# Routed attention with an FFN behind it, one core: a shorter centroid chain, the first one-hot DMAs issued earlier, and three transposes of the fourth pair moved beneath the scores

## The chip, the cores and the metric

One Trainium2 chip, one core. The metric is device time in microseconds (us), the median of several executions. The times of a trace are counted from the start of the span, which is shorter than the time (the profiled execution of the kernel before: span 344.3, time 346.12).

Engines: PE = TensorE, PEld = its weight loads, DVE = VectorE, ACT = ScalarE, POOL = GpSimd, SP = SyncE. "ACTq" and "SPq" in a profile line are issues of DMAs.

## The reference, cut to what matters

```python
batch, n_heads, seq, head_dim, n_clusters = 4, 8, 768, 64, 16
q_assign = argmax(einsum(q_n, c_n)); k_assign = argmax(einsum(k_n, c_n))   # nearest centroid
mask = q_assign[:, :, :, None] == k_assign[:, :, None, :]
attn = softmax(where(mask, scale * q @ k.T, -1e9)); x = attn @ v           # 32 heads
# then, on the 3072 x 512 rows: RMS norm, silu(x @ w_gate) * (x @ w_val) @ w_out
```

The kernel takes two heads at a time ("pairs", 16 in all). The mask is made by 16 extra rows on the contraction: a one-hot of each token's cluster is put below the 64 rows of q and k (tile `aug`, 80 partitions), so a pair's scores can't start before its one-hots are there.

## The kernel before: the parts concerned

Each pair is prepared in thirteen parts: T0 to T3 (three PE transposes each and a copy from PSUM), CAST (bf16 rows of `aug`), SP (assignment matmuls), TR, MX, CMP, SCL, BACK (the one-hot chain, all on DVE), PLACE (DMAs of the one-hots into `aug`), CASTV.

```python
    c_in = const.tile([P, D], F32, name="c_in")
    nc.scalar.dma_start(out=c_in, in_=centroids.rearrange("h c d -> (h c) d"))
    for pi in range(3):
        load_pair(pi, (0, 1))        # q and k, 384 KB each, issued by SP
    load_part(0, 2)                  # v of the first pair
    load_pair(3, (0, 1))
    # ... cut ...
        def place():                 # PLACE: 24 KB each
            ohT = state["ohT"]
            for a in range(2):
                for side in range(2):
                    # ... cut: first pair: ACT issues q's, POOL issues k's ...
                    eng.dma_start(out=aug[st][a][D:KA, side, :].rearrange("c (r n) -> c r n", r=2),
                                  in_=ohT[r:r + 2 * NC, :])
    # ... cut ...
    for i in (TR, MX, CMP, SCL, BACK):
        p0[i]()
    p1[T2](); p1[T3]()
    w_ps = keep_warm(3)              # matmuls of zeros into a scratch bank
    for i in (T0, T2):
        p2[i]()
    p0[PLACE]()
    # ... cut ...
    p3[T0]()
    p3[T1]()                         # needs the fourth pair's k
    keep_warm(2, w_ps)
    load_part(1, 2, nc.scalar)
    p1[SP](); p1[TR](); p1[CAST]()
    keep_warm(3, w_ps)
    # from here on: steps; one step = a score chunk of a head, and what at(step, ...) hangs on it
    for step in range(NT):
        score_chunk(slot, j)         # 3 banks of scores per exp at first
        # ... cut: FFN piece, attention x v, division ...
        extras(step)
```

The softmax here doesn't subtract the row's maximum and nothing guards it: scores larger than these inputs give would overflow.

## Time and profile before

| | kernel before |
|---|---|
| time | 346.56 us, median of 3 (345.97 to 346.69) |
| span of the trace | 344.3 |
| first score matmul, first exp | 16.65, 17.50 |
| first FFN matmul (`gp`) | 64.92 |
| start of the last block of output matmuls (`dp`) | 332.22 |

These four marks cut the span into three stretches. Up to the first exp, loads and preparation decide; from there to the first `gp`, ACT's exps; behind it, PE. Of the third, two waits, in the timeline of PE of the kernel before (start, length, engine, line, operation, operands, count, and in brackets the idle time ahead with its releaser):

```profile
279.50 0.81 PE L402 MATMUL gp<-xnT,wg 128*128 128x384 bf16 x4 [0.44 <-DVE uu L411]
280.62 0.81 PE L402 MATMUL vp<-xnT,wv 128*128 128x384 bf16 x4 [0.32 <-DVE gvT L417]
```

### The profile page before, as it was taken

Reading aid. Unit: us, or ns where it says so; the run is one execution under the profiler, and the core shown is the slowest. Engines: PE = TensorE matmul, PEld = TensorE weight load, DVE = VectorE, ACT = ScalarE, POOL = GpSimd, SP = SyncE. Lnnn points to the kernel's source line nnn. Section 1 sums busy time; section 2 is a strip of 40 time slices with the busy share of each in tenths; the row PEclk is TensorE's granted clock in tenths of the full one; section 3 lists DMA queues with packets and bytes.
Section 4 is the critical chain, followed back from the end, with each engine's and each line's share of the span. In section 5 each row is a group of like instructions: output and inputs, shape, how many; then the busy total and the mean of one; then the engine's idle time right before and its main releaser. Section 6 shows DMA issues by size and latency. Waiting matters only on the chain.

```text
span 344.3 us, 7504 instructions
## 1 busy us (share of the span) xinstructions
PE 332.0 (96%) x2925; PEld 202.9 (59%) x2958; DVE 222.2 (65%) x458; ACT 226.9 (66%) x391; POOL 88.9 (26%) x123
## 2 busy tenths in 40 slices
PE   8899999999999999999999999999999999999995
PEld 3446666667666565666656566666666645555553
DVE  5684788698764778866465567874554677655540
ACT  4489999978777686766767677777777253323322
POOL 2677786066431123230111205010000011000000
PEclk9999999999999999999999999999999999999999
DMA  7665999909943125161501003120000022300012
GB/s 258 211 202 166 260 239 249 267 14 152 228 150 112 69 64 166 42 183 41 170 5 42 32 12 78 38 51 32 32 24 9 32 31 77 78 30 30 32 61 91
DMA packets 36770, 34.98 MB, mean 102 GB/s; under 512 B 13520, under 2 KB 33664, under 8 KB 36736
## 3 DMA queue, kind: packets, MB, share of 16 engines
q1 hardware_dynamic: 30240, 29.20, 27.3%
q0 software_dynamic: 5984, 4.84, 9.3%
q10 hardware_dynamic: 512, 0.48, 0.5%
q8 instruction: 23, 0.38, 0.5%
q14 instruction: 11, 0.09, 0.1%
HBM read 28.61 MB, written 6.29 MB: 101 GB/s over the span
## 4 chain that ended last, share of the span: by engine, by line
PE 84%; DVE 7%; ACT 3%; DMA 3%; issue 2%; POOL 1%; POOLq 0%; DVEq 0%; SPq 0%; ACTq 0%
PE gp L402 17%; PE vp L402 17%; PE dp L435 16%; PE sc L300 12%; PE acc L314 9%; PE tp L196 5%; PE sp L232 3%; PE scw L300 2%; DMA k_in<-in_k_dram 2%; ACT pT L303 2%; PE w_ps L129 1%; DVE qk L200 1%; DVE oh L249 1%; DVE x L324 1%; DVE xn L368 1%
## 5 line engine op out<-in xcount | busy, mean ns | idle before, releaser
L303 ACT ACTIVATE pT<-sc 128x512 bf16<-128x512 f32 x192 | 113.8, 598 | 45.5 <-PE sc L300 44.9
L411 DVE SCALAR_TENSOR_TENSOR uu<-th,gp 128x384 f32<-128x384 f32 x96 | 53.0, 552 | 66.5 <-ACT th L407 66.3
L402 PE MATMUL gp<-xnT,wg 128*128 128x384 bf16 x384 | 78.1, 325 | 0.6 <-DVE uu L411 0.4
L402 PE MATMUL vp<-xnT,wv 128*128 128x384 bf16 x384 | 78.2, 326 | 0.5 <-DVE gvT L417 0.5
L407 ACT ACTIVATE th<-gp 128x384 f32<-128x384 f32 x96 | 47.2, 492 | 43.6 <-PE gp L402 41.0
L314 PEld LDWEIGHTS <-pT 128*128 128x128 bf16 x1152 | 56.8, 97 | 29.4 <-DVE x L324 2.4
L300 PE MATMUL sc<-aug 80*128 80x512 bf16 (+1 forms) x256 | 73.0, 327 | 0.0
L435 PE MATMUL dp<-wo,gvT 128*128 128x512 bf16 (+1 forms) x268 | 71.3, 369 | 1.6
L219 POOL CAST aug<-qk 64x768 bf16<-64x768 f32 x60 | 51.7, 862 | 56.3 <-DVE qk L200 38.2
L314 PE MATMUL acc<-vbf,pT 128*128 128x65 bf16 x1152 | 62.9, 194 | 1.7 <-DVE x L324 0.9
L417 DVE TENSOR_TENSOR gvT<-uu,vp 128x384 bf16<-128x384 f32 x96 | 52.6, 548 | 5.9 <-PE vp L402 0.8
L402 PEld LDWEIGHTS <-wg 128*128 128x128 bf16 x384 | 37.2, 97 | 30.7 <-issue 1.3
L402 PEld LDWEIGHTS <-wv 128*128 128x128 bf16 x384 | 37.1, 97 | 19.1 <-issue 0.9
L303 ACT ACTIVATE pT<-scw 128x1536 bf16<-128x1536 f32 x32 | 44.8, 1457 | 5.1 <-DMA v_in<-in_v_dram 2.4
L435 PEld LDWEIGHTS <-gvT 128*128 128x128 bf16 x300 | 29.1, 97 | 24.4
L300 PEld LDWEIGHTS <-aug 80*128 80x128 bf16 x384 | 33.1, 98 | 17.2 <-issue 7.1
L200 DVE COPY qk<-tp 128x384 f32<-128x384 f32 x38 | 20.7, 553 | 17.0 <-PE tp L196 16.9
L300 PE MATMUL scw<-aug 80*128 80x512 bf16 (+1 forms) x128 | 26.1, 326 | 0.4 <-issue 0.4
L359 POOL TENSOR_SCALAR ir<-ss 128x3 f32<-128x3 f32 x7 | 1.6, 235 | 95.6 <-ACT jk L345 84.0
L368 DVE SCALAR_TENSOR_TENSOR xn<-x,ir,g_b 128x512 bf16<-128x512 bf16 x24 | 20.4, 862 | 6.8 <-POOL ir L360 5.7
L224 POOL CAST vbf<-v_in 128x768 bf16<-128x768 f32 x16 | 13.6, 847 | 34.3 <-issue 33.9
L202 ACT COPY qk<-tp 128x384 f32<-128x384 f32 x26 | 12.3, 479 | 11.0 <-PE tp L196 10.8
(62 smaller groups left out, 217.2 us busy)
## 6 DMA issues: line engine op xcount, KB each, us to landing
q_in<-in_q_dram SPq DMA_DIRECT2D x16, 384.0 KB, 6.1
k_in<-in_k_dram SPq DMA_DIRECT2D x16, 384.0 KB, 6.6
out_dram<-ob SPq DMA_DIRECT2D x23, 256.0 KB, 2.0
v_in<-in_v_dram SPq DMA_DIRECT2D x15, 384.0 KB, 6.4
wg<-in_moe_w_gate_dram POOLq DMA_DIRECT2D x4, 384.0 KB, 8.7
wv<-in_moe_w_val_dram POOLq DMA_DIRECT2D x4, 384.0 KB, 11.4
wo<-in_moe_w_out_dram POOLq DMA_DIRECT2D x4, 384.0 KB, 7.6
aug<-ohT SPq DMA_DIRECT2D x57, 24.0 KB, 1.9
```

Source lines behind the costliest of these rows:

```text
L196: nc.tensor.transpose(tp[:, i * P:(i + 1) * P], src[:, a, i * P:(i + 1) * P], ident_f)
L200: nc.vector.tensor_copy(dst, tp)
L219: nc.gpsimd.tensor_copy(aug[st][a][0:D, :, par * HS:(par + 1) * HS], qk32[0][par * D:(par + 1) * D, 2 * a:2 * a + 2, :])
L300: nc.tensor.matmul(sc[:, o:o + n], lhsT=ag[:, 1, kc * P:(kc + 1) * P], rhs=ag[:, 0, qo:qo + n], start=True, stop=True)
L303: nc.scalar.activation(pts[slot][:, j * CH:(j + nch) * CH], sc[:, :nch * CH], ACT.Exp, scale=scale)
L314: nc.tensor.matmul(acc[:, TORD[g], :], lhsT=pts[slot][:, kc * S + g * P:kc * S + (g + 1) * P], rhs=vb[:, a, TORD[kc], :], start=(kc == 0), ...
L368: nc.vector.scalar_tensor_tensor(st["xn"][:, tl, :], x_t[b][:, t, :], st["ir", m][:, tl:tl + 1], g_b, op0=ALU.mult, op1=ALU.mult)
L402: nc.tensor.matmul(pt[:, :HS], lhsT=w[:, dc, fc * P:(fc + 1) * P], rhs=xnT[b, m][:, :, dc, :], start=(dc == 0), stop=(dc == DC - 1))
L407: nc.scalar.activation(th, pt[:, :HS], ACT.Tanh, scale=0.5)
L411: nc.vector.scalar_tensor_tensor(uu, th, 1.0, pt[:, :HS], op0=ALU.add, op1=ALU.mult)
L417: nc.vector.tensor_tensor(gvT[half][:, fc, :], uu, pt[:, :HS], op=ALU.mult)
L435: nc.tensor.matmul(dp, lhsT=gvT[hf][:, f, tl * P:(tl + 1) * P], rhs=wo[:, f, cols], start=(f == 0), stop=(f == FC - 1))
```

## The change

Its intent: let the first scores start earlier, and keep PE's in-order stream from standing at tiles that the scores don't need (0.51 us at the fourth pair's k tile in the trace of before). The core of the diff (cut: the dummy matmuls, who copies which tile, an extra column of 1e-15 in `c_in` for the sum of squares, the second pair's assignment and transpose, which move from ahead of the scores to step 0, and the third pair's steps, which move to 4 to 18):

```diff
-    for pi in range(3):
+    for pi in range(4):
         load_pair(pi, (0, 1))
     load_part(0, 2)
-    load_pair(3, (0, 1))
@@ centroid chain
-    nc.vector.tensor_mul(c_sq, c_in, c_in)
-    nc.vector.reduce_sum(c_ss, c_sq, axis=AX)
+    nc.vector.scalar_tensor_tensor(c_sq, c_in, 1.0, c_in, op0=ALU.mult, op1=ALU.mult, accum_out=c_ss)
     nc.vector.reciprocal(c_t, c_nm)
-    nc.vector.tensor_mul(c_t, c_t, c_ss)
-    nc.vector.tensor_add(c_nm, c_nm, c_t)
-    nc.vector.tensor_scalar(c_nm, c_nm, scalar1=0.5, scalar2=1e-6, op0=ALU.mult, op1=ALU.add)
-    nc.vector.reciprocal(c_t, c_nm)
-    for i in range(2):
-        nc.vector.tensor_scalar_mul(c2[:, i, :], c_in, c_t)
+    nc.vector.scalar_tensor_tensor(c_t, c_t, c_ss, c_nm, op0=ALU.mult, op1=ALU.add)
+    nc.vector.tensor_scalar_add(c_t, c_t, 2e-6)
+    nc.vector.reciprocal(c_t, c_t)
+    nc.vector.tensor_scalar_mul(c2, c_in[:, 0:D].unsqueeze(1).to_broadcast([P, 2, D]), c_t)
@@ ahead of the scores
-    for i in (T0, T1, T2, T3):
-        p0[i]()
-    put_centroids()
-    p0[CAST]()
+    p0[T0]()
+    p0[T2]()
+    keep_warm(2, w_ps)
+    put_centroids()
+    p0[T1]()
+    p0[T3]()
+    p0[CAST]()
+    for i in (SP, TR, MX, CMP, SCL, BACK, PLACE):
+        p0[i]()
     p3[T0]()
-    p3[T1]()
-    p1[SP]()
-    p1[TR]()
@@ steps
-    for i, step in ((T2, 4), (T3, 7), (SP, 11), (TR, 13), ...):           # p3
+    for i, step in ((T1, 10), (T2, 12), (T3, 15), (SP, 19), (TR, 20), ...):
@@ last batch's RMS norm
-            early = (8, 8, 8, 9, 9, 10, 11) if b == B - 1 else ...
+            early = (8, 8, 9, 9, 10, 11, 12) if b == B - 1 else ...
@@ weight loads
-    for i, step in enumerate((44, 49, 54, 60, 66, 71, 75, 77, 105, 111, 117, 123)):
+    for i, step in enumerate((44, 49, 54, 59, 64, 67, 70, 72, 105, 111, 117, 123)):
```

More of the change, by code (lines that the diff above doesn't have):

```diff
@@ L89, in load_pair @@
             load_part(pi, kind)
-    c_in = const.tile([P, D], F32, name="c_in")
-    nc.scalar.dma_start(out=c_in, in_=centroids.rearrange("h c d -> (h c) d"))
-    for pi in range(3):
+    c_in = const.tile([P, D + 1], F32, name="c_in")
+    nc.vector.memset(c_in[:, D:D + 1], 1e-15)
+    nc.scalar.dma_start(out=c_in[:, 0:D], in_=centroids.rearrange("h c d -> (h c) d"))
+    for pi in range(4):
         load_pair(pi, (0, 1))
     load_part(0, 2)
-    load_pair(3, (0, 1))
     g_b = const.tile([P, DM], F32, name="g_b")
@@ L130, in keep_warm @@
         return w_ps
-    c_sq = const.tile([P, D], F32, name="c_sq")
+    c_sq = const.tile([P, D + 1], F32, name="c_sq")
     c_ss = const.tile([P, 1], F32, name="c_ss")
@@ L191, in t_group @@
                 tp = ((ps_t, ps_pv)[g - 2]).tile([P, HS], F32, name="tp", tag=("t", "acc")[g - 2])
+            elif (pi, g) in late:
+                tp = late[pi, g][:, 0:HS]
             else:
@@ L197, in t_group @@
             dst = qk32[0][:, g, :]
-            on_dve = (g % 2 == 0 if pi == 0 else g > 1 if pi in (1, 3) else g % 2 if pi == 2 else pi < 7 or g % 2)
+            on_dve = (g in (0, 3) if pi == 0 else g == 3 if pi == 2 else pi < 7 or g % 2)
             if on_dve:
@@ L206, in casts @@
             if pi == 0:
-                for g in range(4):
+                for g in (0, 2, 1, 3):
                     a, side = divmod(g, 2)
@@ L471 @@
     p0, p1, p2, p3 = (prep_parts(pi) for pi in range(4))
-    keep_warm(8)
-    for i in (T0, T1, T2, T3):
-        p0[i]()
-    put_centroids()
-    p0[CAST]()
-    keep_warm(3)
-    p0[SP]()
-    p1[T0]()
-    p1[T1]()
-    for i in (TR, MX, CMP, SCL, BACK):
-        p0[i]()
-    p1[T2]()
-    p1[T3]()
-    w_ps = keep_warm(3)
-    for i in (T0, T2):
-        p2[i]()
-    p0[PLACE]()
-    p0[CASTV]()
-    for i in (T1, T3):
-        p2[i]()
-    keep_warm(2, w_ps)
+    w_ps = keep_warm(8)
+    p0[T0]()
[5 more added lines that the diff above has]
+    p0[CAST]()
+    keep_warm(1, w_ps)
+    for i in (SP, TR, MX, CMP, SCL, BACK, PLACE):
+        p0[i]()
+    for i in (T0, T1, T2, T3):
+        p1[i]()
+    late[3, 0] = keep_warm(3)
+    for i in (T0, T2, T1, T3):
+        p2[i]()
     p3[T0]()
-    p3[T1]()
-    keep_warm(2, w_ps)
     load_part(1, 2, nc.scalar)
-    p1[SP]()
-    p1[TR]()
     p1[CAST]()
-    keep_warm(3, w_ps)
+    keep_warm(4)
     first.close()
@@ L503 @@
                                                  reuse_waits="tile"))
-    for i, step in ((MX, 0), (CMP, 1), (SCL, 1), (BACK, 2), (PLACE, 2), (CASTV, 3)):
+    at(2, p0[CASTV])
+    for i, step in ((SP, 0), (TR, 0), (MX, 1), (CMP, 2), (SCL, 2), (BACK, 3), (PLACE, 3), (CASTV, 5)):
         at(step, p1[i])
-    at(3, lambda: load_part(2, 2))
-    at(5, lambda: load_part(3, 2))
+    for i, step in ((T1, 10), (T2, 12), (T3, 15), (SP, 19), (TR, 20), (MX, 21), (CMP, 22), (SCL, 23), (BACK, 24),
+                    (PLACE, 24), (CAST, 24), (CASTV, 28)):
+        at(step, p3[i])
+    for i, step in ((SP, 4), (TR, 5), (MX, 10), (CMP, 12), (SCL, 15), (BACK, 18), (PLACE, 18), (CAST, 6), (CASTV, 14)):
+        at(step, p2[i])
+    for pi in range(2, 4):
+        at(3, lambda pi=pi: load_part(pi, 2))
     at(8, lambda: load_pair(4))
-    for i, step in ((CAST, 3), (SP, 0), (TR, 3), (MX, 5), (CMP, 6), (SCL, 8), (BACK, 9), (PLACE, 9), (CASTV, 10)):
-        at(step, p2[i])
     at(22, lambda: load_pair(5))
@@ L521 @@
         else:
-            early = (8, 8, 8, 9, 9, 10, 11) if b == B - 1 else (9, 9, 10, 11, 12, 13, 15)
+            early = (8, 8, 9, 9, 10, 11, 12) if b == B - 1 else (9, 9, 10, 11, 12, 13, 15)
             plan = [(sumsq, early[:3], (0, 1, 2)), (inv, early[3:4], (0,)), (norm, early[4:], (0, 1, 2)),
@@ L527 @@
                 at(H * NCH * (b + 1) + step, lambda fn=fn, it=it, more=more: fn(it, *more))
-    for i, step in ((T2, 4), (T3, 7), (SP, 11), (TR, 13), (MX, 14), (CMP, 15), (SCL, 16), (BACK, 18), (PLACE, 18),
-                    (CAST, 18), (CASTV, 28)):
-        at(step, p3[i])
     at(30, lambda: load_pair(6))
```

## The prediction

> **What bounds the kernel now.** I read the page first, then the chain of waits that ended last, then the timeline of the first 18 us, then the ACT timeline up to 68 us, then the end (266 to 298 us). The page's part 1 gives the two busiest engines:
>
> ```profile
> PE 332.0 (96%) x2925; PEld 202.9 (59%) x2958; DVE 222.2 (65%) x458; ACT 226.9 (66%) x391; POOL 88.9 (26%) x123
> ```
>
> PE is busy for 96% of the span, but that is an average. Most of the change lies before the first scores, and there the chain in order of time shows something else:
>
> ```profile
> 6.54 7.43 DMA k_in<-in_k_dram
> ...
> 13.97 0.14 issue
> 14.11 0.52 PE tp L196 x3
> 14.63 0.43 PE w_ps L129 x2
> 15.06 0.85 PE sp L232 x8
> ```
>
> (Columns: start us, length us, what.) The end of the kernel is tied to the arrival, at 13.97 us, of the fourth pair's k tile. PE takes its instructions in order, so its transposes of that tile, some dummy matmuls [...] and the second pair's assignment all stand ahead of the first score. The timelines show the same wait from ACT's and PE's side:
>
> ```profile
> 14.11 0.52 PE L196 MATMUL tp<-ident_f,k_in 128*128 128x128 f32 x3 [0.51 <-DMA k_in<-in_k_dram]
> 15.78 0.82 PE L129 MATMUL w_ps<-zeros 128*128 128x512 bf16 x3
> 16.65 0.81 PE L300 MATMUL scw<-aug 80*128 80x512 bf16 x4
> ...
> 17.50 1.45 ACT L303 ACTIVATE pT<-scw 128x1536 bf16<-128x1536 f32 x1 [2.35 <-DMA v_in<-in_v_dram]
> ```
>
> The bracket names a v load as ACT's releaser, but that load is only issued by ACT; the exp needs the score matmuls that began at 16.65, so I read it as "waits for PE". From there to 65 us there is a second regime, bound by ACT, with 32 exps of 1.4 us almost back to back (columns: start, length, groups, idle before):
>
> ```profile
> 17.50 5.68 ACT L303 ACTIVATE pT<-scw 128x1536 bf16<-128x1536 f32 x4 [2.35 <-DMA v_in<-in_v_dram]
> 23.88 8.30 ACT L303 ACTIVATE pT<-scw 128x1536 bf16<-128x1536 f32 x6 [0.70 <-PE scw L300]
> 32.43 4.45 ACT L303 ACTIVATE pT<-scw 128x1536 bf16<-128x1536 f32 x3 [0.24 <-PE scw L300]
> ```
>
> The holes are 0.70 once and about 0.25 us per two or three heads' exps. After 65 us PE is the bound and its order is fixed, so what is won before the first exp should reach the end, if ACT stays fed and nothing waits for the weights.
>
> [...] PE stands 0.51 us for the fourth k tile although the first pair's one-hots do not need it. [...] So issuing the fourth pair's q and k ahead of v should bring them about one tile earlier. The trace has 320 to 396 GB/s from 5 to 11 us; by that, a 384 KB tile takes some 1.05 us, and the last two arrivals that PE waited for (13.05 and 13.97) are 0.92 apart, which fits. [...] The trace has 2.4 to 2.8 us from issue to landing for the first pair's 24 KB one-hots. [...] The 128x1 steps of the centroid chain take 150 to 160 ns, and start every 0.20 us, so each one removed is worth 0.20.
>
> **The change, part by part.**
>
> Centroid chain. Now: square 3.08, sum 3.34, POOL's power 3.71 to 4.27, then five steps of 0.20 us from 4.30, and two multiplications (0.42) that end at 5.70. After: square and sum in one (I estimate 0.3 from the row of 0.23 and a short accumulator read), which takes away about 0.2; one step fewer after the power, 0.20; the two multiplications as one 128x128, an estimate of 0.27 for 0.42, 0.15. Sum 0.55: the scaled centroids are ready at 5.15 instead of 5.70. PE reaches the centroid transpose at 4.69 + two groups of three transposes (0.39 and 0.33) + two dummies (0.43) = 5.84, against 6.21 now. The transpose takes 0.27, the copies to the block-diagonal tile follow at 6.19 and 6.48 and end at 6.77 (now 7.14).
>
> But this 0.37 isn't passed on. DVE must then copy T3 (k of the pair's second head), whose transposes now stand behind the centroids on PE: 6.28 to 6.77, the copy 6.81 to 7.33, then two casts of 0.56 each to 8.45. The first stream transpose of the one-hot chain starts behind these: 8.47, where it now starts at 8.32. The chain behind it lasts 8.32 to 11.03 = 2.71 us, so the one-hots are ready at 11.18 instead of 11.03. I count the shorter chain as a loss of 0.15 by itself: it pays for the rearrangement.
>
> One-hot DMAs ahead of ACT's copies. ACT now issues its two at 11.56, behind two copies that began at 11.17; after, at 11.22. POOL issues at 11.34 now (0.31 behind the one-hots), 11.49 after. With the 2.8 us to landing that the first POOL one took, the first head's rows are there at 14.0 (ACT) and 14.3 (POOL). In the kernel before they were there at about 14.4, over 2 us ahead of the scores at 16.65: this was hidden. It becomes the bound now.
>
> Three transposes of the fourth pair beneath the scores. Only T0 (q, first head) stays ahead of them. PE after: assignment to about 8.1; second pair's transposes, held by its k tile until 8.97, and three dummies to 10.65; third pair's q to 11.3; its k only once DVE has copied the second pair's first tile (DVE now copies all four, from 11.2), so 11.85 to 12.5; the fourth pair's q, which comes before v in the queue and should be there at about 12 to 12.5; then four dummies of 0.216. PE is ready at 13.7. ACT, which copies three tiles of the third pair behind its two DMA issues (1.3 us, to 12.5), needs 3 x 0.48 and is done at 13.95; the first scores' PSUM banks need one of these copies. So three arrivals: 13.7 PE, 13.95 ACT, 14.3 DMA. The latest decides; with a little for the wait itself the first score matmul begins at 14.4 and the first exp 0.85 later (16.65 to 17.50 now): 15.3. That is 17.50 - 15.3 = 2.2 us won.
>
> From 15 to 65 us. The three transposes and copies (0.33 us of PE, 0.55 of DVE each) are now done between the scores, with two 3-bank score buffers of slack. Taken off that stretch: the transposes at steps 4 and 7, behind which the second exp row stood 0.70 us idle. Put in: T1, T2 and T3 at steps 10, 12, 15, each of which needs the single transpose bank that DVE must first have emptied. I expect 0.3 of the 0.70 to remain: 0.4 won. The weight loads are issued up to five steps earlier, as they must; the eight that the first FFN pieces need landed by about 71 us, chunk by chunk ahead of their use, and no PE wait names them. I count 0.
>
> The end. The last batch's third sum of squares and the norms come one step later, so one more DVE step is done before DVE stands 1.69 us for POOL's power. PE now loses 0.44 + 0.32 us there (gp at 279.50, vp at 280.62). One wait should go, but two norms of 0.75 now follow each other directly and another should come. I count 0.
>
> Sum: 346.56 - 2.2 - 0.4 = 343.96, say 343.9 us.
>
> **The rivals.** First, that the one-hot chain is the bound and later than I think: if a 0.55 us copy more lies ahead of the stream transpose on DVE, or POOL's DMA takes 3.3 us (the longest of those seen in the first 20 us), either makes the first exp about 0.5 later, both together 16.3 and the result 344.9. For it: DVE is 93% busy or more from 5 to 12 us. Against: its order is known and I counted it.
>
> Second, that ACT's regime absorbs it. The second pair's one-hots must land before the seventh exp; I put their transpose at 18.5 and their landing at 21 to 22.6, while the scores want them at about 22.3. POOL now has the second pair's casts and a v cast (four of 0.86 and 0.84) ahead of those DMAs. If they are late, ACT stands. This would cost up to 1 us: 345.
>
> Third, that more is won: PE's in-order blocking is also what makes the 0.70 and some of the 0.25 holes, and the end may lose its 0.76. All of it would make 342.8.
>
> Fourth, that the loads are what ends last anyway: if the fourth q tile still lands at 13.05 (its order in the queue changed nothing), PE is ready at 14.3, the same as the one-hots, and the result moves by 0.1 only. So this one is cheap.
>
> **Range and chances.** The rivals reach from 342.8 to 345; with 0.3 us of scatter between runs (345.97 to 346.69 now) I take 342.5 to 345.4. Faster by over 2% would need 339.6, that is 6.9 us, more than the whole wait from 11 to 17.5 us could give: 2%. Slower by over 2%: 1%. Within 2%: 97%.
>
> **What would show it.** Right: the first exp at 15.0 to 15.7; the first score's LDWEIGHTS released by a one-hot DMA or an ACT copy, and no wait for the k load in the chain; the first stream transpose no earlier than 8.3; the last scw exp ending some 2.3 to 2.9 us earlier; the first gp matmul near 62.3 instead of 64.92; the distance from there to the end unchanged within 0.4. Wrong: a first exp after 16.5, or a first exp at 15 with a hole of over 1 us at the seventh exp or a wait on a weight load, which would mean the win was handed back. If the stream transpose starts at 7.9, I have mis-sized DVE's part and the win is nearer 3.

## The result, and the profile after

The changed kernel took 344.26 us (median of 4, 343.94 to 344.86), the kernel before, beside it, 346.62 (4 runs, 345.97 to 347.32). The ratio is 0.9934, 95% interval 0.9909 to 0.9958. A ratio here is always the mean time of one kernel's runs over that of the other's in the same rounds, so it isn't quite the ratio of the medians. The verdict is "same" at 2%: 0.7% faster.

The profiled execution was the slowest of the four (344.86), so its span, 343.1, shows half of the gain only. Its page, part 1:

```profile
PE 333.1 (97%) x2955; PEld 203.1 (59%) x2955; DVE 222.6 (65%) x460; ACT 225.5 (66%) x388; POOL 89.2 (26%) x123
```

Against the same line of before nothing stands out, as it must be: the change moves waits of 1 us in a span of 344. The chain in order of time answers the lines that the prediction shows of before (start, length, what):

```profile
10.55 0.59 DVE ohT L259
11.14 0.30 issue
11.44 3.68 DMA aug<-ohT
15.12 0.05 issue
15.17 0.82 PE scw L299 x4
```

The arrival of the fourth k tile is gone from the chain. In its place stands the transfer of the first pair's one-hots, 3.68 us. PE's timeline shows from the other side what that costs:

```profile
12.67 1.03 PE L129 MATMUL w_ps<-zeros 128*128 128x512 bf16 x4
15.17 0.82 PE L299 MATMUL scw<-aug 80*128 80x512 bf16 x4 [1.48 <-DMA aug<-ohT]
```

PE was through with its dummies at 13.70 and stood 1.48 us. ACT's timeline, to be held against the exp lines of before:

```profile
16.03 9.98 ACT L302 ACTIVATE pT<-scw 128x1536 bf16<-128x1536 f32 x7 [2.27 <-PE scw L299]
26.83 4.13 ACT L302 ACTIVATE pT<-scw 128x1536 bf16<-128x1536 f32 x3 [0.82 <-PE scw L299]
31.53 4.45 ACT L302 ACTIVATE pT<-scw 128x1536 bf16<-128x1536 f32 x3 [0.57 <-PE scw L299]
```

The first exp starts 1.47 earlier. But the 0.70 hole ahead of the fifth exp has not shrunk: it is now ahead of the eighth and 0.82 long, and the next hole has grown from 0.24 to 0.57. At the end:

```profile
284.77 0.81 PE L401 MATMUL gp<-xnT,wg 128*128 128x384 bf16 x4 [0.38 <-DMA xnT<-xn]
```

Both waits of before (0.76) are gone, and one of 0.38 has come. The sum by stretches, for this pair of traces and for a second pair, of unchanged copies on one chip (`r_before`, `r_after`, below), in us:

| stretch | before, after | r_before, r_after | predicted |
|---|---|---|---|
| start to first exp | 17.50, 16.03: -1.47 | 18.47, 16.77: -1.70 | -2.2 |
| first exp to first `gp` | 47.42, 48.21: +0.79 | 47.43, 47.92: +0.49 | -0.4 |
| first `gp` to last `dp` block | 267.30, 266.94: -0.36 | 267.29, 266.87: -0.42 | 0 |
| rest of the span (given to 0.1) | 12.1, 11.9: -0.2 | 12.1, 11.9: -0.2 | 0 |
| span | 344.3, 343.1: -1.2 | 345.3, 343.5: -1.8 | -2.6 |

So the number was right and two of its terms were not. The experiments ask where these two went.

### The profile page after: what moved, and what is told of

The parts are those of the page before. It is cut to its first block, busy times and chain, and to the rows that moved or that the text cites.

```text
span 343.1 us, 7530 instructions
## 1 busy us (share of the span) xinstructions
PE 333.1 (97%) x2955; PEld 203.1 (59%) x2955; DVE 222.6 (65%) x460; ACT 225.5 (66%) x388; POOL 89.2 (26%) x123
## 4 chain that ended last, share of the span: by engine, by line
PE 86%; DVE 6%; ACT 3%; DMA 2%; issue 1%; POOLq 0%; POOL 0%; DVEq 0%; ACTq 0%
PE gp L401 17%; PE vp L401 17%; PE dp L434 17%; PE sc L299 12%; PE acc L313 9%; PE tp L195 5%; PE scw L299 3%; PE sp L231 3%; ACT pT L302 2%; PE w_ps L129 1%; DMA xnT<-xn 1%; DMA aug<-ohT 1%; DVE oh L254 1%; DVE tr L238 1%; DVE qk L199 1%
## 5 line engine op out<-in xcount | busy, mean ns | idle before, releaser
L434 PE MATMUL dp<-wo,gvT 128*128 128x512 bf16 (+1 forms) x300 | 75.9, 370 | 0.0
L199 DVE COPY qk<-tp 128x384 f32<-128x384 f32 x40 | 21.8, 552 | 15.6 <-PE tp L195 15.4
L323 DVE TENSOR_TENSOR x<-acc,inv 128x384 bf16<-128x384 f32 x32 | 17.8, 557 | 1.1
```

Source lines behind the costliest of these rows:

```text
L199: nc.vector.tensor_copy(dst, tp)
L323: nc.vector.tensor_tensor(x_t[b][:, :, h * D:(h + 1) * D], acc[:, :, 0:D], inv.to_broadcast([P, ST, D]), op=ALU.mult)
L434: nc.tensor.matmul(dp, lhsT=gvT[hf][:, f, tl * P:(tl + 1) * P], rhs=wo[:, f, cols], start=(f == 0), stop=(f == FC - 1))
```

## The experiments

The theories, with the letters that the expectations use:

- **A**: the one-hots land late because ACT issues a second v load right behind them (at 12.58, before: 14.67), which is in flight with them (it landed at 16.0).
- **E** (formed when A fell): they land late because of the loads issued ahead of them, last of all the first pair's v, which the change moves behind the fourth pair's q and k.
- **C**: the stretch of the exps gives back because the second pair's one-hot chain starts later on DVE (16.84 instead of ahead of the scores).
- The rival to C: a single DVE operation runs long there because POOL is at work on its casts, and with it the division that frees PE's accumulator comes late.

Where an expectation uses another letter, it says with it what it holds. The first four kernels ran on one chip (before: 346.54, 11 runs).

### Unchanged copies: r_before and r_after

> The kernel before again, unchanged, for a second trace. Both theories: first exp at 17.5 +- 0.3 us, the first pair's one-hot DMAs 2.4 to 2.9 us from issue to landing, first gp matmul at 64.9 +- 0.4. If these move by more than 0.5 us from trace to trace, single traces are too coarse for the sums below.

> The changed kernel again, unchanged, for a second trace and five more rounds. Expected: ratio to before 0.993 +- 0.002; first exp 16.0 +- 0.3; one-hot DMAs 3.3 to 3.8 us to landing; ACT holes of about 0.8 before the eighth and 0.6 before the eleventh exp; first gp at 64.2 +- 0.4.

Before: 347.08 (one run). After: 344.77 (6 runs, 344.43 to 345.28), ratio 0.9953 [0.9941, 0.9965]. Both traces have a later start than the first pair: the first one-hot stream transpose at 9.35 and 9.37, not 8.32 and 8.43. PE's timeline of the kernel before, first the given trace, then this one (the second and third of the first four groups of three transposes):

```profile
5.17 0.55 PE L196 MATMUL tp<-ident_f,k_in 128*128 128x128 f32 x3
5.56 0.49 PE L196 MATMUL tp<-ident_f,q_in 128*128 128x128 f32 x3
```

```profile
5.33 0.88 PE L196 MATMUL tp<-ident_f,k_in 128*128 128x128 f32 x3
6.00 0.85 PE L196 MATMUL tp<-ident_f,q_in 128*128 128x128 f32 x3
```

The same instructions follow each other every 0.39 us in one execution and every 0.67 in the other. The kernel is not what differs: over all fourteen traces the first stream transpose starts anywhere from 8.04 to 9.67. What differs, as I read it, is when PE gets its full clock. Each trace's record of the granted clock begins, at full clock, somewhere between 4.04 us (`sp1_first`, stream transpose 8.04) and 7.35 (`div_first`, 9.67); it is 4.76 and 7.23 in these two traces. (The page counts the time ahead of that record as full clock, so its row doesn't show this. A group of three transposes took 0.85 to 0.90 us where `p_t1`, below, has a recorded clock of 0.50.) The two traces of the kernel before differ by 1.03 us at the stream transpose and by 1.0 in span, and both first exps, 18.47 and 16.77, missed what was expected of them. So single traces may only be compared stretch by stretch. (The single timed run of `r_before`: its mean clock was as in the others.)

### Theory A: v1_late

```diff
-    load_part(1, 2, nc.scalar)
@@ behind first.close()
+    at(0, lambda: load_part(1, 2, nc.scalar))
```

> The changed kernel with the second pair's v load issued by ACT after the first exp instead of ahead of it (about 16 us instead of 12.58). Theory A (the one-hot DMAs land 0.9 us later than I took because this 384 KB load and the first v load, moved to the end of the queue, are in flight with them): landing comes down from 3.7 to 3.0 or less, first exp at 15.3. Rival B (the loads of the first four pairs alone do it, or the DMAs vary anyway): landing stays at 3.3 to 3.8 and the first exp at 16.0. Time: A up to 0.7 us less than the changed kernel, if the stretch up to 65 us does not give it back; B the same.

344.33 (342.42 to 344.58), ratio 0.9931 [0.9913, 0.9949]; against `r_after` that is 0.2% less, and the two intervals overlap. The second v load was now issued at 15.46, far behind, and ACT's one-hots, issued at 10.81, still needed 3.6 us:

```profile
14.60 0.82 PE L299 MATMUL scw<-aug 80*128 80x512 bf16 x4 [1.05 <-DMA aug<-ohT]
```

A has fallen. But what was landed in this trace just before? The first pair's v, issued by SP at 6.87, at 14.2; the one-hots at 14.4 (ACT) and 14.5 (POOL). That made me look at the same pair of times in the traces at hand, and form theory E.

| trace | one-hots issued (ACT, POOL) | last earlier load landed | one-hots landed |
|---|---|---|---|
| before | 11.56, 11.34 | 14.0 (fourth k) | 14.3, 14.2 |
| after | 11.16, 11.44 | 14.7 (first v) | 14.9, 15.1 |
| v1_late | 10.81, 11.09 | 14.2 (first v) | 14.4, 14.5 |

The packets of the traces say a little more. In after the one-hots' packets begin to move 1.3 us after their issue, amid those of the loads, and most of them (58 of ACT's 64 and 29 of POOL's 32, counting both heads) start ahead of the last load packet; the rest, and the landing, come with the end of the loads. So they don't queue behind the loads as a whole.

### Theory C: sp1_first

```diff
     keep_warm(4)
+    p1[SP]()
+    p1[TR]()
@@ step list of the second pair
-    ((SP, 0), (TR, 0), (MX, 1), ...)
+    ((MX, 1), ...)
```

(SP's tile comes from the single transpose bank, as the first six banks are about to be given away.)

> The changed kernel with the second pair's assignment matmuls and first DVE transpose ahead of the first scores (into the single transpose bank), where PE stands 1.48 us and DVE 2.95 us. Theory C (the stretch from 16 to 65 us gives 0.8 us of the early start back because DVE begins the second pair's chain only at 16.84, then has chains of three pairs, three copies and the first division in one row without a gap until 31 us): DVE begins that transpose at 14.7, the hole of 0.82 before the eighth exp and that of 0.57 before the eleventh shrink to 0.3 in all, the first exp stays at 16.0 and the first gp comes at 63.4; time 0.8 us less than the changed kernel. Rival D (the holes come from POOL's casts slowing DVE, or from buffers, not from when the chain begins): first gp at 64.2 and the same time within 0.3.

343.92 (342.89 to 344.37), ratio 0.9926 [0.9913, 0.9939], an interval that doesn't meet that of `r_after`. The second pair's chain starts two microseconds earlier on DVE:

```profile
14.77 0.58 DVE L238 STREAM_TRANSPOSE tr<-sp 128x384 f32<-128x384 f32 x1 [1.08 <-PE sp L231]
```

First exp to first `gp` took 47.54, against 48.21 in the given trace of after and 47.92 in `r_after`; the first seven exps took 9.57 instead of 9.98. But the holes ahead of the eighth and eleventh exps stayed (0.76 and 0.55). C is right for about 0.4 us (the first seven exps take 9.56 or 9.57 in all three traces with this edit and 9.97 or 9.98 in the eight of the changed start without it) and doesn't explain the holes.

### Undoing parts of the change: u_chain, u_place, u_tail

These and `p_t1` ran on a second chip (before: 346.26, 345.89 to 347.81).

`u_chain` puts the old centroid chain back into the changed kernel.

> The changed kernel with the old centroid chain (two DVE steps and one small multiplication more). My step in the prediction: the shorter chain is hidden behind PE's transposes and DVE's casts, so undoing it makes the centroid transpose and the copies behind it later by about 0.1 to 0.2 us; first one-hot stream transpose at 8.5 to 8.7 instead of 8.43, first exp 16.1 to 16.3, time within 0.3 us of the changed kernel. Rival: the chain sets the start, then all of its 0.55 us shows: stream transpose at 9.0, time 0.5 more.

344.29 (343.02 to 345.26), ratio 0.9935 [0.9911, 0.9958]: the ratio of the whole change. In its trace the scaled centroids were ready at 5.57 and the stream transpose started at 8.76 (after: 5.35 and 8.43). The 0.3 us are not the old chain's doing: PE's first six transposes took 1.21 us instead of 0.89 in this execution, and PE reached the centroid transpose at 6.17, well behind the ready centroids, as it does in after (5.85). From the start of the square to the scaled centroids the old chain takes 2.62 us and the new one 2.12, but neither is waited for: in the new order of work the shorter chain shows no gain. The one-hots landed at 13.9 and 14.1, behind the end of the loads (13.7). The first score of that trace waited for a copy of DVE, not for the one-hots, and the first exp came at 15.16. A hole of 1.05 us ahead of the tenth exp is taken up under `div_first`.

`u_place` issues ACT's one-hot DMAs behind ACT's copies again.

```diff
-    for i in (SP, TR, MX, CMP, SCL, BACK, PLACE):
+    for i in (SP, TR, MX, CMP, SCL, BACK):
         p0[i]()
@@ ahead of p3[T0]()
+    p0[PLACE]()
```

> The changed kernel with the first pair's one-hot DMAs issued by ACT and POOL after ACT's three copies of the third pair instead of ahead of them. If the one-hot DMAs are the bound of the first score now: ACT issues at 12.6 or later instead of 11.16, first score 1 to 1.5 us later, first exp 17.0 to 17.6, and time 0.7 to 1.4 us more than the changed kernel. Rival (ACT's side is hidden behind POOL's DMA, which lands last): first exp 16.0 to 16.3, time the same.

344.80 (343.68 to 347.46; one far run), ratio 0.9967 [0.9939, 0.9996], not told apart from the whole change. ACT issued its one-hots at 12.14 instead of 11.16, and they landed at 14.4, behind a v load that landed at 13.9; POOL's, issued as before, landed at 14.0. The first exp came at 15.34, so neither the 17.0 to 17.6 expected nor the rival's 16.0 to 16.3. A full microsecond of earlier issue gains some 0.3 us of landing at most, and nothing that the time shows, while the loads are under way. (The far run, 347.46, has a mean granted clock of 0.995.)

`u_tail` gives the last batch's RMS norm its old steps, (8, 8, 8, 9, 9, 10, 11).

> The changed kernel with the last batch's sums of squares and norms at their old steps. The traces of before and after lose 0.8 and 0.4 us of PE in that stretch, so 0.3 to 0.4 us more than the changed kernel and the two PE waits on DVE (uu, gvT) back; my prediction counted 0. Rival: the wait for the DMA transpose (0.38 us, new) takes over in either case, time the same.

344.57 (344.12 to 344.84), ratio 0.9942 [0.9925, 0.9958], which the time doesn't tell from the whole change. The trace does: first `gp` to last `dp` block took 267.28. The three traces with the old steps up to here give 267.29, 267.30 and 267.30, those of the changed kernel and of `v1_late` and `sp1_first` 266.87 to 266.94. The later steps are worth 0.4 us there; in the other traces with them it is 266.40 to 266.73, as the new wait of 0.38 is shorter or gone.

This trace has a second, unplanned finding. Its hole ahead of the eighth exp is 0.21, as if the change had kept its promise, though nothing there was touched. The DVE timelines of after and of `u_tail` at that place:

```profile
23.66 0.56 DVE L199 COPY qk<-tp 128x384 f32<-128x384 f32 x1 [0.28 <-PE tp L195]
24.14 0.90 DVE L254 TENSOR_SCALAR oh<-oh 64x384 bf16<-64x384 bf16 x1
24.96 0.18 DVE L322 RECIPROCAL inv<-acc 128x6 f32<-128x6 f32 x1
25.17 0.56 DVE L323 TENSOR_TENSOR x<-acc,inv 128x384 bf16<-128x384 f32 x1
```

```profile
23.45 0.56 DVE L199 COPY qk<-tp 128x384 f32<-128x384 f32 x1 [0.24 <-PE tp L195]
23.92 0.24 DVE L254 TENSOR_SCALAR oh<-oh 64x384 bf16<-64x384 bf16 x1
24.09 0.18 DVE L322 RECIPROCAL inv<-acc 128x6 f32<-128x6 f32 x1
24.31 0.56 DVE L323 TENSOR_TENSOR x<-acc,inv 128x384 bf16<-128x384 f32 x1
```

The scaling of the third pair's one-hots, 64x384 in bf16, takes 0.24 us in one execution and 0.90 in the other. Behind it stands the division, which frees PE's accumulator, and so PE stands in the first case (timeline of PE, after):

```profile
25.78 0.36 PE L313 MATMUL acc<-vbf,pT 128*128 128x65 bf16 x6 [0.54 <-DVE x L323]
```

At that time POOL makes the third pair's four casts of `aug`, 0.83 us each if nothing lengthens them. Here are the third and fourth of them (x2 is for both), in after, in `u_tail` and, from the last experiment below, in `v0_sp1`:

```profile
24.10 1.71 POOL L218 CAST aug<-qk 64x768 bf16<-64x768 f32 x2
```

```profile
23.92 1.81 POOL L218 CAST aug<-qk 64x768 bf16<-64x768 f32 x2
```

```profile
23.32 1.71 POOL L217 CAST aug<-qk 64x768 bf16<-64x768 f32 x2
```

In after, the third cast (24.10 to 24.93) started 0.04 us ahead of the scaling, and the scaling ended at 25.04, 0.11 behind that cast. In `v0_sp1` the cast took 23.32 to 24.15, the scaling 23.58 to 24.26 (0.68), again 0.11 behind it. In `u_tail` both started at 23.92, the scaling ran at its 0.24, and it was POOL's two casts that took 0.1 longer. In eleven of the fourteen traces a cast was under way when this scaling started, and the scaling ended 0.11 us behind it each time, up to 0.90 long. In the other three (`u_chain`, `u_tail`, `v0_act`) the two started within 0.02 us of each other; the scaling took its 0.24 and the cast 0.91 to 0.93 instead of 0.82. The hole follows: 0.21 in these three, 0.60 with a scaling of 0.68 (`v0_sp1`), 0.76 with 0.83 (`sp1_first`), 0.81 to 0.82 with 0.89 or 0.90. Whether it is 0.2 or 0.8 us is decided by some hundredths of a microsecond.

### The k tile alone: p_t1

The kernel before, with only the fourth pair's T1 moved, to step 3, where it meets the old steps of T2 (4) and T3 (7).

```diff
-    p3[T1]()
@@ step list of the fourth pair
-    for i, step in ((T2, 4), (T3, 7), ...
+    for i, step in ((T1, 3), (T2, 4), (T3, 7), ...
```

> The kernel before with one thing changed: the fourth pair's first k transposes go from ahead of the scores to step 3 beneath them (their copy on DVE). If the wait for that k tile (13.97 us) is what set the first score before: first score at about 15.5 instead of 16.65, held now by the rest of what stands ahead of it on PE (the q tile at 13.05, second pair's assignment, five dummies), first exp 16.4, time 0.6 to 1.1 us less than before, if the next stretch keeps it; one transpose more beneath the scores may take back 0.3. Rival (the one-hots or ACT set it anyway): first exp over 17.2, same time.

346.84 (346.5 to 348.72), ratio 1.0017 [0.9994, 1.0039]: nothing is won. The trace has both halves of the story. First exp at 16.16, that is 1.34 earlier than before: the k tile was the bound of the start. Then ACT (timeline):

```profile
16.16 2.99 ACT L303 ACTIVATE pT<-scw 128x1536 bf16<-128x1536 f32 x2 [2.30 <-PE scw L300]
22.22 1.45 ACT L303 ACTIVATE pT<-scw 128x1536 bf16<-128x1536 f32 x1 [3.07 <-PE scw L300]
...
27.02 12.66 ACT L303 ACTIVATE pT<-scw 128x1536 bf16<-128x1536 f32 x9 [1.43 <-PE scw L300]
```

and PE:

```profile
18.80 0.55 PE L196 MATMUL tp<-ident_f,k_in 128*128 128x128 f32 x3 [1.14 <-DVE tr L239]
20.00 0.90 PE L196 MATMUL tp<-ident_f,q_in 128*128 128x128 f32 x3 [0.65 <-DVE qk L200]
```

The transposes now stand in PE's order ahead of scores that ACT needs, and wait for their one bank, which DVE, behind with the second and third pair's chains, hasn't emptied. First exp to first `gp` took 51.58 instead of 47.42. But not all of these 4.2 us are the order of work. This trace is of the slowest execution by far (348.72; the other five took 346.5 to 346.89), and its TensorE clock fell. The views of two stretches (busy time of PE, PEld, DVE, ACT and POOL with instructions, then granted clock, DMA share, GB/s), and the same score group before and in the dip:

```profile
16.33:19.74 3.41, 1.89 (x15) 0.62 (x7) 2.70 (x5) 2.73 (x2) 2.33 (x5) 1.00 0.04 9
19.74:23.15 3.41, 3.15 (x12) 2.15 (x13) 2.38 (x5) 0.93 (x1) 3.25 (x5) 0.50 0.88 259
```

```profile
16.84 0.82 PE L300 MATMUL scw<-aug 80*128 80x512 bf16 x4
20.70 1.49 PE L300 MATMUL scw<-aug 80*128 80x512 bf16 x4
```

The clock stayed at 0.50 until 26.56. Half of these 6.8 us, 3.4, is the most that this can have cost (my estimate); no such dip is in the trace of the kernel before. An estimate for a usual execution is the 1.34 won at the start plus the 0.6 by which the median is above that of the kernel before: some 1.9 us given back. So where the transposes go decides whether the start that is won is kept; step 3 loses it. That step 10 is the right place was not tested by itself.

### Theory E, and the third division: v0_act, div_first, all_three

A third chip (before: 346.9, 345.91 to 348.01).

`v0_act` takes the first pair's v out of SP's queue; ACT issues it where it issued the second pair's, which goes to step 0.

```diff
-    load_part(0, 2)
@@
-    load_part(1, 2, nc.scalar)
+    load_part(0, 2, nc.scalar)
@@ behind first.close()
+    at(0, lambda: load_part(1, 2, nc.scalar))
```

> The changed kernel with the first v load taken from the end of the sync queue and issued by ACT behind the one-hot DMAs (where the second v load stood, 12.6 us), and the second v load issued by ACT after the first exp. Theory E (in ten traces the one-hots, whenever issued, from 10.8 to 12.4 us, landed 0.0 to 0.5 us after the last load that had been issued before them, so that load is what the first score waits for): the last load ahead of them is now the fourth k tile at about 13.2, the one-hots land at 13.3 to 13.7, first score at about 14.0, held by PE and DVE, first exp at 14.9 (counted for a trace whose first stream transpose is at 8.4), time 0.5 to 1 us less than the changed kernel. Rival (fixed landing time of 2.2 to 3.8 us that depends on the chip): landing stays over 3.3 where the changed kernel has it, first exp as in the changed kernel, same time.

343.06 (342.0 to 346.03; the far run with a mean clock of 0.995), ratio 0.9901 [0.9868, 0.9935]. This execution had a late start (stream transpose 9.65), and the one-hots were ready only at 12.35; ACT's then landed 1.9 us after their issue and POOL's 2.0, and PE didn't wait for them: the first score came at 15.21 behind ACT's copies.

`div_first` lets the divisions go ahead on DVE: SCL of the third pair from step 15 to 17, SCL, BACK and PLACE of the fourth from 23 and 24 to 26.

> The changed kernel with the scaling of the third pair's one-hots (step 15) and of the fourth pair's, with its transpose back (23, 24), moved behind the division of the head just finished (steps 17 and 26). Theory F (the stretch from first exp to first gp lasts 47.9 to 48.2 us in four traces of the changed start against 47.4 before because these one-hot steps, held to 0.73 to 0.90 us by POOL's casts, stand on DVE ahead of the division that frees the accumulator for PE): the holes of 0.82 before the eighth and 0.56 before the eleventh exp fall to about 0.25 each, first exp to first gp 47.3 or less, time 0.6 to 0.9 us less than the changed kernel. Rival: the holes come from the single transpose bank; then they stay, 47.9 to 48.2, same time.

344.73 (342.86 to 347.48), ratio 0.9949 [0.991, 0.9989]. The hole ahead of the eighth exp is 0.21, as intended. But three new ones of 2.01, 1.05 and 0.69 us came, and PE's timeline gives the first of them another cause:

```profile
29.80 0.52 PE L195 MATMUL tp<-ident_f,q_in 128*128 128x128 f32 x3 [2.00 <-DMA q_in<-in_q_dram]
```

The fifth pair's q, issued at 22.34, landed 7.3 us later; it took 4.6 to 5.0 in twelve other traces, and 6.2 in `u_chain`, whose steps are not moved; there the hole ahead of the tenth exp is PE standing 1.04 us ahead of the transposes of that tile, which landed at 27.8, 0.1 before they began (the view names DVE's `ohT`, which ended at the same time). So a late load doesn't need the moved steps. The other two holes have a further cause: behind the wait of 2.00 the granted clock was 0.50 from 31.24 to 34.65. Its six times scatter over 4.6 us, which is more than those of any other version here; the two slowest (346.88, the profiled one, and 347.48) have a mean clock of 0.995, the other four (342.86 to 345.33) 0.999 or more. As a test of the theory it is inconclusive.

`all_three` joins `v0_act`, `div_first` and `sp1_first`.

> Both of these and the second pair's assignment ahead of the first scores. If E and F hold and add to the 0.6 us of that one: first exp at 14.9, first gp 47.0 later at 61.9, time 1.5 to 2.3 us less than the changed kernel, ratio to before 0.988 to 0.990. If the parts hide one another, as little as 0.8 us less.

343.04 (342.7 to 344.34), ratio 0.9903 [0.9879, 0.9928]. This trace had an early start, and its one-hots were issued at 10.87 and 11.14, like those of after and `v1_late`. They landed 2.9 and 2.8 us later, at 13.7 and 13.9, right behind the fourth k tile (13.6), while the v load issued behind them landed at 15.6. With the v load ahead of them it was 3.5 to 3.8 in those two. E fits all fourteen traces: in eleven the first head's one-hots landed 0.2 to 0.5 us behind the last load issued ahead of them, and in the other three (`v0_act`, `v0_sp1`, `div_first`), where that load was in early, 1.9 to 2.0 us after their issue. `div_first` has v ahead of them as the change has it, so what counts is when the loads end, not v as such. This trace also has the better test of the third division: its scaling took 0.60 us, and with the division ahead of it the hole ahead of the eighth exp was 0.21.

### Without the moved divisions: v0_sp1

> The combined version without the moved divisions (SCL, BACK and PLACE at the steps of the changed kernel): first v load behind the fourth pair's q, second pair's assignment and stream transpose ahead of the first scores. If theory C in the part that held is right (the second pair's chain earlier is worth 0.4 to 0.7 us of the stretch) and the moved divisions are worth nothing sure, one-hots land no more than 3 us after issue, the stretch from first exp to first gp is 47.2 to 47.6, and the ratio to the kernel before is 0.988 to 0.991 (combined version: 0.990). If the moved divisions were what carried the combined version, the stretch is 47.9 or more, a 0.8 us hole stands before the eighth exp, and the ratio is 0.992 or more. Start of the one-hot chain may again differ by over 1 us between executions.

A fourth chip (before: 346.44, 346.04 to 347.53): 343.42 (342.94 to 343.48), ratio 0.991 [0.9896, 0.9923]. First exp to first `gp` 47.46, within the expectation; the hole ahead of the eighth exp 0.60, with the scaling at 0.68. The moved divisions are worth nothing that shows in the time (0.3 us between the two traces). The chain of waits no longer has the one-hots' DMA in it:

```profile
12.24 0.88 PE tp L194 x6
13.12 0.33 PE w_ps L194 x3
13.45 0.22 PE w_ps L128
13.66 0.05 issue
13.71 0.59 PE w_ps L128 x2
14.31 0.78 PE sp L230 x8
15.09 0.77 PE scw L298 x4
```

They were issued at 11.78 and 12.05 and landed at 13.7 and 14.1, 1.9 and 2.0 us later, with the last load in at 13.2. PE now goes without a stop from its third pair's transposes into the scores. `v0_act`, `all_three` and `v0_sp1` can't be told from each other; by their ratios all three are about 1% faster than the kernel before (0.9901, 0.9903, 0.991), the change 0.5 to 0.7% (0.9953, 0.9934). That these were other chips leaves a little room; the interval of `v0_sp1` and that of `r_after` don't meet. But it does meet that of `sp1_first`, so what taking v out adds to the time is not shown apart. Nor does all of the gain come from the start: the first exps of these three traces (16.06, 15.49, 15.88) are not earlier than those of `u_chain` and `u_place` (15.16, 15.34), while first `gp` to last `dp` block takes 266.40 to 266.42, since PE's wait for the transfer of `xnT` (0.08 to 0.39 in the seven traces with v in SP's queue and the new steps) is gone. No run says why.

## Why the prediction was right, and which of its steps were not

**The bound before: right.** The fourth k tile was what the first score waited for: taken away by itself (`p_t1`), the first exp comes 1.34 earlier.

**Centroid chain: right.** Ready at 5.35 (put at 5.15), stream transpose at 8.43 (put at 8.47), later than before as it said. The chain itself got 0.50 us shorter (put at 0.55), and `u_chain` shows no gain from that: PE comes later than it in either kernel.

**One-hots ready and issued: right.** The one-hots were done at 11.14 (11.18), issued at 11.16 by ACT (11.22) and 11.44 by POOL (11.49).

**Their landing: the step that failed in the first term.** The prediction took 2.8 us "that the first POOL one took" and landed them at 14.3; it was 3.8 and 3.7 us, 14.9 and 15.1. Its other two arrivals were met: PE ready at 13.70 (13.7), ACT at 13.76 (13.95). So the start won 1.5 to 1.7, not 2.2. The 2.8 us were no property of the transfer (1.9 to 2.0 in `v0_act`, `v0_sp1` and `div_first`). They were the distance from the issue to the end of the loads ahead. The change made v the last of these loads, and it landed at 14.7 (`r_after`: 15.5), where the last had landed at 14.0 (14.9). With the same order of loads `u_chain` and `u_place` had v at 13.7 and 13.9 and the first exp at 15.16 and 15.34, as predicted: how much of the 2.2 us comes differs by execution or chip, and why the loads end earlier there stays open. Rival 1 had a landing of 3.3 us and the right place; the fourth rival, that "the loads are what ends last anyway", had the right mechanism, but looked for it in the q tile, which did come at 12.2 as the main line said.

**From 15 to 65 us: failed in sign.** Predicted 0.4 won, measured 0.5 to 0.8 given back (0.1 won in `u_tail` and `v0_act`, where the scaling named below was short). Of the 0.79 in the given pair, 0.57 are there by the end of the thirteenth exp (19.38 us after the first exp's start before, 19.95 after). "I expect 0.3 of the 0.70 to remain" named the transposes as the cause of the hole; with these gone from there it reappeared behind another wait, DVE's division behind a scaling that ended 0.11 us behind a cast of POOL and took 0.90 us (in `u_tail` it took 0.24, and the hole was 0.21). Some 0.4 more are the later chain of the second pair (`sp1_first`), which rival 2 had named, though it looked for the loss at the one-hots' landing. The two overlap, so I don't add them.

**Weights: right.** No weight load is among PE's waits after.

**The end: failed by 0.4, in the kernel's favour.** "One wait should go, but two norms of 0.75 now follow each other directly and another should come" is what happened; but two went (0.44 and 0.32) and the new one is 0.38 (0.08 to 0.39 over seven traces). The count of 0 was short of 0.76 - 0.38 = 0.38, and `u_tail` gives it back.

**Its signs:** the stream transpose at 8.43, the release of the first score by a one-hot DMA and no k load in the chain came as it said. The first exp (16.03, said 15.0 to 15.7), the first `gp` (64.24, said near 62.3) and the distance from there to the end (0.6 shorter, said unchanged within 0.4) did not.

**The sum** came out right partly by luck, as the errors cancel in part: 0.5 to 0.7 too much at the start, 0.9 to 1.2 too much in the middle, against 0.4 too little at the end and 0.2 in the rest leaves 0.8 to 1.4 too much in these two pairs of traces. The timed result (344.26 for 343.9) came closer than the traces, as the start's scatter of over 1 us falls differently in each execution; in `r_after` the gain was 0.5%.

**Open:** why the full clock begins at different times at the start; why the one-hots count as landed only behind the earlier loads, most of their packets having gone before; what delayed the fifth pair's q in `div_first` and `u_chain`; and whether PE's waits brought the clock down in `p_t1` and `div_first`.

## What to carry to other kernels

A small transfer that is on the path should be read together with the loads that were issued ahead of it: issuing it 1 us earlier won some 0.3 us of landing at most, while with one 384 KB load taken out from ahead of it the first score waited for it in none of three traces, and in five of the eight that had that load there (it landed 1.0 to 1.6 us behind the load ahead of it). Work that is moved off the start has to go where its buffer's reader is idle: a transpose group won 1.3 us at the start and lost all of it again at step 3, and the change, with its steps from 10 on, gave back 0.5 to 0.8 of 1.5 to 1.7. Look at the granted clock, stretch by stretch, before a loss is read from one trace: in `p_t1` and `div_first` it was 0.50 in just the stretch in question. And before a small DVE operation is put ahead of one that frees a PSUM bank, look what POOL does at that time: with a cast under way the scaling of 0.24 us took up to 0.90.

## What the traces show of the hardware, without a reason

- The landing of a small transfer: most packets of the first pair's 24 KB one-hots started ahead of the last packet of SP's 384 KB loads (58 of ACT's 64 and 29 of POOL's 32 in after), but they counted as landed 0.2 to 0.5 us behind the last load issued ahead of them in eleven of fourteen traces, up to 3.9 us from their issue. In the other three (`v0_act`, `v0_sp1` and `div_first`) they landed 1.9 to 2.0 us from their issue. No run tests the reason.
- The granted clock: the record of the full clock began 4.04 to 7.35 us into the span, with the dummies from 1.30 us on in all traces: a spread of 3.3 us. In the two traces with a dip the stretches at one clock (13.65 and 6.83 us in `p_t1`, 23.89 and 3.41 in `div_first`) are 4, 2, 7 and 1 times 3.41. The clock fell to 0.50 behind 3.41 us in which PE was busy for 1.89 (`p_t1`) and 1.36 (`div_first`), and stayed full behind 3.41 us with 2.04 (after, 11.65 to 15.06). Two dips are few, and no run was made to test this.
- A DVE operation beside a cast of POOL: the scaling of 0.24 us on DVE ended 0.11 us behind the cast of POOL that had started ahead of it, after up to 0.90, in eleven of fourteen traces.
- The spread of the same loads: the fifth pair's q took 4.6 to 5.0 us from issue to landing in twelve traces, 6.2 and 7.3 in the other two, and v, as the last load ahead of the one-hots, landed anywhere from 12.9 to 15.5 us in eight.
